# Block transposes on VectorE for the first keys and queries, v in a new token order, and another order of steps

## The chip, the core and the metric

The kernel runs on one core of a Trainium2 chip. The time is the device time of one execution in microseconds; several executions are run and their median is given. A profile is one further execution, recorded instruction by instruction. The core has four compute engines that the text speaks of: TensorE (matmuls, "PE" in the profile, with weight loads as "PEld"), VectorE ("DVE"), ScalarE ("ACT") and GpSimd ("POOL"). SyncE ("SP") issues most DMA transfers, ScalarE and GpSimd issue some.

## The reference

Two layers, one after the other. The first is an attention with polynomial features; the second a feed-forward layer (FFN) whose activation is a ratio of polynomials.

```
batch, n_heads, seq, head_dim = 4, 4, 1088, 32;  r = 8
phi(x):  a = S1 @ x ;  b = S2 @ x ;  outer product of a and b: 64 features
kv  = sum over tokens of phi(k) v^T       (64 x 32 per head)
z   = sum over tokens of phi(k)           (64 per head)
out = (phi(q) kv) / (phi(q) z + 1e-6)     -> x, 4352 tokens x 128

h = x @ w_in                              (128 -> 2048)
P = a0 + a1 h + a2 h^2 + a3 h^3
Q = 1 + |b0| |h| + |b1| h^2
y = (P / (Q + 1e-6)) @ w_out              (2048 -> 128)
```

## The kernel before

**Tiling.** Each of the 4 batches has 1024 main tokens and a remainder of 64. The main tokens of a batch are two chunks of 512 tokens; the remainders of all batches form a last, ninth chunk. A chunk's tokens lie over the 128 partitions with token = 8 p + j, so that a chunk takes four values of j (`JC = 4`).

**Keys, per batch (`add_keys`).** `features` works on one chunk: TensorE transposes four 128x128 f32 tiles of k (one per head, four tokens with their 32 dimensions each; line 420), ScalarE copies the result out of PSUM (line 425), TensorE multiplies with S12, which holds S1 and S2 transposed, in a block-diagonal form (line 430), ScalarE copies a and b out (line 438), VectorE forms the 64 products (line 449). Then TensorE accumulates kv and z over the tokens with v as the other operand (line 466; v has a column of ones for z). After the second chunk and the remainder, VectorE writes kv into block-diagonal form (`kv_bd`, lines 510 and 514) and z into `z_bd` (518); one more matmul with `S2x` (line 523) and two VectorE products (529, 532) turn z into extra columns of the query projection, so that denominators come out of it.

**Queries, per chunk (`add_queries`).** Transposes (555), copy (560), projection (566), copy (577), for all chunks but the first the denominators (588 to 600), the product (605), transposes of the product (613), copy (620) and a matmul with `kv_bd` (626) that gives x transposed. The first chunk is `early`: it doesn't wait for z, but takes numerators and denominators from one set of matmuls (634), divides on VectorE (645 to 655) and transposes x after that (663, 669).

**FFN (`add_group`).** Groups of up to eight blocks of 128 hidden units for one chunk: h in PSUM (line 748), ScalarE copies it to bf16 (`hb`, 754), VectorE and ScalarE form the ratio (the reciprocal of Q as exp(-ln Q), lines 784 and 787), TensorE multiplies with w_out (807). Sixteen groups add some terms by DMAs that accumulate, issued by GpSimd (844). The four groups of kind "s" (4, 7, 11, 15) take |b0| |h| from ScalarE: after each of the four 128x1024 pieces of h is copied, an Abs with scale is run on the same PSUM tile (759).

**Start.** Ten matmuls of zeros keep TensorE busy from the first microsecond (326). SR, S1 and S2 with a copy per head, is loaded to 16 partitions, transposed by TensorE (339), copied by VectorE (347) and masked into S12 (348); `S2x` comes from a matmul with `sel` (343) and a VectorE copy (352). The first batch's k, q and v come in two loads each, 512 bytes in a run; v goes to a spare buffer and GpSimd copies it into `v_aug[0]` (404).

**Order.** Every piece of work is a step of a plan. The list `ORDER` gives the order in which all steps issue their instructions, and so the order on each engine and each DMA queue; waits between engines follow from the data and the buffers. A DMA of SP also waits for the landing of the one issued eight before it (ScalarE's loads at the start count too).

## Time and profile before

| | us |
|---|---|
| median of 3 runs | 268.0 (266.77 to 268.14) |
| the profiled execution's own time | 270.2 |
| its span, first to last instruction | 268.5 |
| TensorE busy | 246.2 (92%) |
| VectorE busy | 244.1 (91%) |
| ScalarE busy | 242.7 (90%) |
| GpSimd busy | 38.2 (14%) |
| first FFN matmul starts | 20.51 |
| last compute instruction ends | 264.5 |

A row of instructions gives start, duration, engine, line, operation, the tiles written and read, shapes and a count, and in brackets the idle time before it with what ended it. A row of the groups by form ends with the group's busy time, the mean of one in ns, and the idle time before. A row of a stage gives its bounds and length, the busy time of TensorE, its weight loads, VectorE, ScalarE and GpSimd, TensorE's granted clock as a share of the full one, the DMA engines' busy share and GB/s.

### The profile page before, as it was taken

The page shows a single profiled execution, that of the slowest core. Times are in us where ns is not written, and L with a number is a line of the kernel's source. Part 1 is how long each engine was busy: PE and PEld are TensorE (multiplying, and loading weights), DVE is VectorE, ACT ScalarE, POOL GpSimd, SP SyncE. Part 2 cuts the span into 40 slices and gives each one's busy share as a digit, 9 for nine tenths or more (in the row PEclk, how much of TensorE's full clock was granted, in tenths as well). Part 3 has the DMA queues.
Part 4 walks back from the last instruction along what each step waited for, and adds up shares of the span by engine and source line. Part 5 has one row for each costly group of instructions (what it writes and reads, how often), then busy time and mean ns, then how long its engine had stood idle before and what let it go on. Part 6 is the DMA issues. An engine that isn't in the chain of part 4 may idle for free.

```text
span 268.5 us, 2984 instructions
## 1 busy us (share of the span) xinstructions
PE 246.2 (92%) x1099; PEld 137.5 (51%) x1113; DVE 244.1 (91%) x234; ACT 242.7 (90%) x218; POOL 38.2 (14%) x58
## 2 busy tenths in 40 slices
PE   8999999999999999999999989999999879778653
PEld 4974567755665645466546434445344334634241
DVE  1643999799999999999999999999999999999992
ACT  2437978899999999999999999999999999999972
POOL 4800001100202101202020302020211202101000
PEclk9997999999999999999999999999999999997995
DMA  6797849980394996296949893959599799897511
GB/s 183 200 294 150 152 100 201 177 172 2 42 114 53 105 171 136 44 121 68 124 76 121 143 172 34 123 88 110 64 123 186 121 138 116 117 99 111 64 39 61
DMA packets 38718, 31.66 MB, mean 118 GB/s; under 512 B 16816, under 2 KB 34992, under 8 KB 38576
## 3 DMA queue, kind: packets, MB, share of 16 engines
q0 software_dynamic: 14144, 20.45, 58.9%
q1 hardware_dynamic: 23792, 10.89, 16.0%
q10 hardware_dynamic: 768, 0.14, 0.3%
q8 instruction: 9, 0.15, 0.2%
q14 instruction: 5, 0.04, 0.0%
HBM read 8.79 MB, written 2.23 MB: 41 GB/s over the span
## 4 chain that ended last, share of the span: by engine, by line
PE 42%; DVE 23%; ACT 23%; issue 6%; DMA 4%; DVEq 0%; ACTq 0%; POOLq 0%
PE h_ps L748 20%; DVE y L780 11%; ACT hb L754 8%; ACT u L787 6%; ACT L L784 5%; PE out_ps L807 5%; PE kv_ps L466 5%; DMA u<-lin 4%; DVE u L780 3%; PE w_ps L430 2%; DVE lin L861 2%; PE out_ps L326 2%; DVE lin L776 2%; DVE y L791 1%; PE w_ps L626 1%
## 5 line engine op out<-in xcount | busy, mean ns | idle before, releaser
L748 PE MATMUL h_ps<-xT,w_in_sb 128*128 128x512 f32 (+1 forms) x288 | 128.3, 581 | 3.8 <-ACT hb L754 3.1
L748 PEld LDWEIGHTS h_ps<-xT,w_in_sb 128*128 128x128 f32 x288 | 52.3, 192 | 54.5 <-issue 40.4
L754 ACT CAST hb<-h_ps 128x1024 bf16<-128x1024 f32 (+1 forms) x70 | 73.6, 1067 | 2.3 <-PE h_ps L748 1.9
L780 DVE TENSOR_TENSOR y<-y,hb 128x4096 bf16<-128x4096 bf16 (+3 forms) x42 | 70.3, 1686 | 0.1
L784 ACT ACTIVATE L<-u,one_ap 128x4096 f32<-128x4096 bf16 (+3 forms) x23 | 66.8, 2906 | 2.4 <-DVE u L780 1.4
L787 ACT ACTIVATE u<-L 128x4096 bf16<-128x4096 f32 (+3 forms) x23 | 64.7, 2812 | 0.1
L780 DVE TENSOR_TENSOR y<-y,u 128x4096 bf16<-128x4096 bf16 (+3 forms) x23 | 40.0, 1739 | 0.2
L807 PEld LDWEIGHTS <-w_out 128*128 128x128 bf16 x224 | 22.1, 100 | 35.0 <-issue 15.0
L844 POOL DMA_DIRECT2D y<-zeros x12 | 19.3, 1612 | 128.1 <-DVE y L780 82.3
L807 PE MATMUL out_ps<-y,w_out 128*128 128x512 bf16 x124 | 30.5, 379 | 0.9 <-DVE y L780 0.5
L780 DVE TENSOR_TENSOR u<-lin,u 128x4096 bf16<-128x4096 bf16 (+3 forms) x19 | 30.8, 1622 | 0.1
L807 PE MATMUL out_ps<-u,w_out 128*128 128x512 bf16 x86 | 23.0, 401 | 4.9 <-ACT o_sb L812 2.7
L791 DVE TENSOR_SCALAR y<-hb,a_sb 128x4096 bf16<-128x4096 bf16 (+3 forms) x19 | 19.3, 1013 | 2.9 <-ACT hb L754 1.9
L776 DVE TENSOR_SCALAR lin<-u,b_abs 128x4096 bf16<-128x4096 bf16 (+3 forms) x19 | 19.2, 1011 | 0.0
L771 DVE TENSOR_SCALAR u<-hb 128x4096 int16<-128x4096 int16 (+3 forms) x19 | 16.9, 890 | 2.2 <-ACT hb L754 2.2
L759 ACT ACTIVATE u<-h_ps,b_abs 128x1024 bf16<-128x1024 f32 x16 | 18.4, 1152 | 0.0
L466 PEld LDWEIGHTS kv_ps<-v_aug,k_p 128*128 128x128 f32 x128 | 15.2, 192 | 1.4 <-DVE y L780 0.8
L466 PE MATMUL kv_ps<-v_aug,k_p 128*128 128x66 f32 x128 | 15.4, 271 | 0.0
L620 ACT COPY q_pT<-w_ps 128x512 f32<-128x512 f32 (+1 forms) x18 | 11.5, 647 | 2.7 <-PE w_ps L613 2.7
L844 POOL DMA_DIRECT2D u<-lin x4 | 5.2, 1311 | 52.7 <-DVE lin L865 26.3
L613 PEld LDWEIGHTS w_ps<-ident,q_p 128*128 128x128 f32 x68 | 8.2, 143 | 8.0 <-ACT q_pT L620 3.6
L449 DVE TENSOR_TENSOR k_p<-ab 128x1024 f32<-128x1024 f32 x8 | 9.6, 1224 | 2.5 <-ACT ab L438 2.5
(100 smaller groups left out, 222.8 us busy)
## 6 DMA issues: line engine op xcount, KB each, us to landing
y<-zeros POOLq DMA_DIRECT2D x11, 1024.0 KB, 11.6
u<-lin POOLq DMA_DIRECT2D x4, 1024.0 KB, 8.3
y<-lin POOLq DMA_DIRECT2D x4, 1024.0 KB, 8.4
out_dram<-oT SPq DMA_DIRECT2D x8, 256.0 KB, 2.4
kq<-in_k_dram SPq DMA_DIRECT2D x3, 512.0 KB, 7.7
v_aug<-in_v_dram SPq DMA_DIRECT2D x12, 128.0 KB, 5.7
kq<-in_q_dram SPq DMA_DIRECT2D x3, 512.0 KB, 4.6
w_in_sb<-in_moe_w_in_dram SPq DMA_DIRECT2D x1, 1024.0 KB, 6.3
```

The costliest lines, as they stand in the source:

```text
L466: nc.tensor.matmul(T["kv", b][:, hp * 66:(hp + 1) * 66], lhsT=lhs(hp), rhs=rhs(hp), start=(first and hp == 0), stop=final, skip_group_chec ...
L748: nc.tensor.matmul(T["h", g, s][:, i * W:(i + 1) * W], lhsT=w_in_sb[:, fi * 128:(fi + 1) * 128], rhs=T["xT", n][:, :W], start=True, stop=True)
L754: nc.scalar.copy(out=T["hb", g][:, s * W:(s + nsub) * W], in_=T["h", g, s][:, :nsub * W])
L759: nc.scalar.activation(out=T["u", g][:, s * W:(s + nsub) * W], in_=T["h", g, s][:, :nsub * W], func=ACT.Abs, scale=b_abs[:, 0:1] if square ...
L771: nc.vector.tensor_scalar(out=u().bitcast(mybir.dt.int16), in0=hb().bitcast(mybir.dt.int16), scalar1=0x7FFF, scalar2=None, op0=AX.bitwise_and)
L776: nc.vector.tensor_scalar(out=lin(), in0=u(), scalar1=b_abs[:, 1:2], scalar2=b_abs[:, 0:1], op0=AX.mult, op1=AX.add)
L780: return lambda: nc.vector.tensor_mul(out=out(), in0=in0(), in1=in1())
L784: nc.scalar.activation(out=T["L", g, l0][:, :lw], in_=T["u", g][:, l0:l0 + lw], func=ACT.Ln, bias=one_ap)
L787: nc.scalar.activation(out=T["u", g][:, l0:l0 + lw], in_=T["L", g, l0][:, :lw], func=ACT.Exp, scale=-1.0)
L791: nc.vector.tensor_scalar(out=y(), in0=hb(), scalar1=a_sb[:, 3:4], scalar2=a_sb[:, 2:3], op0=AX.mult, op1=AX.add)
L807: nc.tensor.matmul(T["o", n][:, :W], lhsT=W_terms[w][:, fis[i], :], rhs=T[src, g][:, i * W:(i + 1) * W], start=(start and i == 0), stop=(s ...
L844: nc.gpsimd.dma_start(out=dst(), in_=src(), accum_op=AX.add, max_dma_last_dim=4096)
```

## The change

- In batches 0 and 1 (`HALVED`) a chunk is 512 consecutive tokens, loaded on its own. Within a key chunk of these, and a query chunk of batch 0 (`Q_BLOCKS`), one VectorE instruction transposes all 32x32 blocks of the loaded tile straight into `kT` or `qT`; TensorE's transposes and ScalarE's copies of those chunks are gone. The projections then give the tokens in another order, partition = token modulo 128.
- v of these batches is loaded in that order, one load per head and chunk: eight loads per batch of 64 KB each, in runs of 128 bytes, straight into `v_aug`; GpSimd's copies are gone. The first two stores of the output write in that order.
- S1 and S2 are loaded to all 128 partitions and transposed by VectorE; `S2x` is a GpSimd copy. `mask4` is made first.
- Nine matmuls of zeros in place of ten at the start, and two and one more behind the two transposes of the first x (`XWARM`).
- In the groups of kind "s", Abs runs once over the whole 128x4096 `hb` in place of four times over PSUM; `hb` is free only after it.
- `ORDER` is a new list. Among other things the first query load is issued ahead of v's, the z projection stands before the first numerators and the second query projection before the first FFN matmul on TensorE; on VectorE the second chunk's denominators and query product come before the first FFN work.

```diff
+    XWARM = (2, 1)
+    ZEROS = 9
+    HALVED = (0, 1)
+    Q_BLOCKS = (0, 1)
...
-    SR = consts.tile([2 * R, H, D], FP, name="SR")
+    SR = consts.tile([128, 2, D], FP, name="SR")
...
+        if b in HALVED:
+            c = part
+            src = src[b, :, c * CW:(c + 1) * CW, :]
+            if name == "v_sb":
+                for h in range(H):
+                    QUEUE[eng].dma_start(out=v_aug[b % 2][:, h, c * JC:(c + 1) * JC, 0:D],
+                                         in_=src[h].rearrange("(a m) d -> m a d", a=JC))
+                return
...
+            QUEUE[eng].dma_start(out=T[name, b][:, :, c * JC:(c + 1) * JC, :],
+                                 in_=src.rearrange("h (p j) d -> p h j d", j=JC))
...
-    ld["v", 0] = load("SP", lambda e: load_main(e, "v_sb", v, 0, 0), 256, rank=-97, take=["q_p"])
-    ld["q", 0] = load("SP", lambda e: load_main(e, "q_sb", q, 0, 0), 256, rank=-96.8, take=["kq"])
-    ld["v", 0, 1] = load("SP", lambda e: load_main(e, "v_sb", v, 0, 1), 256, rank=-96.6)
+    ld["q", 0] = load("SP", lambda e: load_main(e, "q_sb", q, 0, 0), 256, rank=-97, take=["kq"])
+    ld["v", 0] = load("SP", lambda e: load_main(e, "v_sb", v, 0, 0), 512, H, rank=-96.8, take=["v_aug"])
+    ld["v", 0, 1] = load("SP", lambda e: load_main(e, "v_sb", v, 0, 1), 512, H, rank=-96.6)
...
     def s_spread():
-        nc.vector.tensor_copy(out=sT, in_=T["sT"][:, :2 * R])
...
+        nc.vector.transpose(out=sT.rearrange("p s d -> p (s d)"), in_=SR.rearrange("p s d -> p (s d)"))
...
     def s_expanded():
-        nc.vector.tensor_copy(out=S2x, in_=T["s2"][:, :128])
+        nc.gpsimd.tensor_copy(out=S2x, in_=SR[:, 1, None, :].broadcast_to([128, H, D]))
...
+            def block_transposes():
+                T["kT", key] = tile_of(att, "kT", [128, CW], FP)
+                half = T["k_sb", b][:, :, key[1] * JC:(key[1] + 1) * JC, :]
+                nc.vector.transpose(out=T["kT", key].rearrange("p (h m j) -> p h j m", h=H, j=JC), in_=half)
...
+            warm(XWARM[t])
...
+        def s_abs():
+            T["u", g] = tile_of(moe, "u", [128, GW], BF)
+            nc.scalar.activation(out=T["u", g][:, :gw], in_=T["hb", g][:, :gw], func=ACT.Abs, scale=b_abs[:, 0:1])
...
-            p = plan.add("DVE", tt, mul(y, y, hb), after=[p], rank=g - 0.3, give=["hb"], name=f"n2 {g}")
+            p = plan.add("DVE", tt, mul(y, y, hb), after=[p, ha], rank=g - 0.3, give=["hb"], name=f"n2 {g}")
```

## The prediction

> **What bounds the kernel now.** I read the page's engine shares first (TensorE 92%, VectorE 91%, ScalarE 90%: no engine has much room), then the busy time by stage, to see where each engine still has room.

> ```profile
> core 0: us, PE busy (x) PEld busy (x) DVE busy (x) ACT busy (x) POOL busy (x), PEclk, DMA share, GB/s
> 0.00:20.51 20.51, 18.94 (x121) 14.38 (x121) 8.07 (x20) 7.11 (x15) 8.79 (x38) 1.00 0.84 224
> 20.51:27.00 6.49, 6.49 (x16) 3.26 (x17) 2.82 (x8) 4.49 (x6) 0.00 (x0) 0.74 0.70 151
> 27.00:50.00 23.00, 22.89 (x124) 15.44 (x126) 20.99 (x35) 19.95 (x30) 2.53 (x2) 1.00 0.76 149
> 50.00:60.00 10.00, 9.84 (x47) 6.17 (x46) 9.63 (x16) 9.38 (x7) 0.00 (x0) 1.00 0.97 194
> 60.00:150.00 90.00, 89.71 (x395) 50.16 (x400) 89.41 (x69) 89.77 (x80) 11.71 (x8) 1.00 0.70 89
> 150.00:245.00 95.00, 85.15 (x302) 40.18 (x308) 94.88 (x60) 95.00 (x69) 13.86 (x9) 0.99 0.88 119
> 245.00:264.50 19.50, 13.20 (x102) 7.94 (x101) 18.34 (x32) 17.00 (x17) 1.29 (x1) 0.94 0.33 57
> 264.50:268.50 4.00, 0.00 (x0) 0.00 (x0) 0.00 (x0) 0.02 (x1) 0.00 (x0) 0.50 0.21 64
> ```

> The first number of a row is its length, the fourth VectorE's busy time. From 60 to 245 us VectorE idles 0.7 of 185 us. Nearly all its idle time, 24.4 of 268.5 us, lies at the start: 12.4 before the first FFN matmul (20.51), 3.7 up to 27, 2.0 up to 50, then 0.4 + 0.7 + 1.2 and the 4.0 of the last store. So I use a ledger: span = VectorE's work + VectorE's idle time. Work taken from ScalarE or TensorE alone shortens nothing from 60 us on; work given to VectorE lengthens it, unless it fills an early hole.

> The order of time shows what sets the start:

> ```profile
> 0.85 4.43 PE L326 MATMUL out_ps<-const-float32-0.0 128*128 128x512 bf16 x10 [0.85 <-PEq L1019]
> 5.42 1.76 PE L420 MATMUL w_ps<-ident,kq 128*128 128x128 f32 x8
> 6.57 1.24 ACT L425 COPY kT<-w_ps 128x512 f32<-128x512 f32 x2 [4.48 <-PE w_ps L420]
> 7.21 1.10 PE L430 MATMUL w_ps<-S,kT 128*128 128x64 f32 x8
> 8.76 1.23 DVE L449 TENSOR_TENSOR k_p<-ab 128x1024 f32<-128x1024 f32 x1 [2.18 <-ACT ab L438]
> 16.09 0.29 DVE L510 TENSOR_TENSOR kv_bd<-kv_ps,mask 128x128 f32<-128x128 f32 x1 [2.88 <-PE kv_ps L466]
> 17.72 0.17 DVE L645 TENSOR_SCALAR den<-w_ps 128x8 f32<-128x8 f32 x1 [0.77 <-PE w_ps L634]
> ```

> TensorE transposes the keys after its ten warm-up matmuls, ScalarE copies them out, and only at 7.21 does the projection start; the key sums end at 16.06, x is ready and the first FFN matmul starts at 20.51.

> Rows for costs come from the groups by form:

> ```profile
> L333 DVE MEMSET zeros<- 128x512 f32 x1 | 0.5, 485 | 0.1
> L605 DVE TENSOR_TENSOR q_p<-abc 128x512 f32<-128x512 f32 x1 | 0.7, 690 | 0.0
> L449 DVE TENSOR_TENSOR k_p<-ab 128x1024 f32<-128x1024 f32 x8 | 9.6, 1224 | 2.5 <-ACT ab L438 2.5
> L759 ACT ACTIVATE u<-h_ps,b_abs 128x1024 bf16<-128x1024 f32 x16 | 18.4, 1152 | 0.0
> L787 ACT ACTIVATE u<-L 128x4096 bf16<-128x4096 f32 x15 | 56.0, 3737 | 0.0
> ```

> **The change, part by part.**

> *VectorE's work.* Six block transposes of 128x512 f32 are added (four key chunks, two query chunks). The trace has none. Bounds: 0.485 us (the memset of as many elements) and 1.224 us (the product that writes twice as many). I take 0.69, the f32 product of the same 512 elements, since a transpose too reads and writes each element once. Sum 4.1 us. The S2x copy (0.29) leaves VectorE; sT's copy becomes a small transpose (0.17 to about 0.22). Work: 244.1 + 4.1 - 0.29 + 0.05 = 248.0 us.

> *Other engines.* TensorE loses 24 transposes (six groups of four at 0.44 on the chain, 2.6 us) and the two small matmuls from SR, and gains net two warm-up matmuls. ScalarE loses six copies of about 0.6 us and trades 16 x 1.152 = 18.4 us of Abs from PSUM for 4 x 3.74 = 15.0 us from SBUF (priced by the 4096-wide Exp): 7.1 us in all. GpSimd loses the two v copies (0.61 and 1.40). All of it lies beside a full VectorE: worth 0 in the ledger, though it guards VectorE against waits. If VectorE were not full there, ScalarE's 7.1 us would count. The merged Abs is a new wait for the accumulate-DMA behind it on GpSimd's queue and for VectorE's y*hb: for group 4 I put its end near 40 us, and VectorE's own scaled square, which the same DMA needs, near 41, so it hides; if it came late, the DMA (10.5 us on the chain here) would be late by as much, and Ln after it, but VectorE has other groups to work on. The stores of the first two chunks go in 512-byte rows in place of 2 KB, beside work.

> *Start, up to the key sums.* S comes in 256 packets in place of 64; issued by 1.8, with a landing of 2.4 (k's first half took 3.0 with far more bytes) it is there at 4.2, and with transpose and mask product S12 near 4.7 (6.03 before). Then on VectorE: two key transposes (to 5.4 and 6.1) and the query transpose, which waits for a load that takes the place of v's first half in SP's queue; that one let SP go on at 7.18 here, so about 6.8 to 7.5. Were q later, the first key product, queued behind it on VectorE, and with it the key sums would be late by as much. Projections on TensorE 5.6, 6.7, 7.8 to 8.9 (1.10 each); ScalarE's evictions 0.4; VectorE's products 7.5, 8.7, 9.95 to 11.2 (1.23 each). Key sums need v in 128-byte packets: loads one to four are issued by about 5, and land by 8; five to eight queue behind the landing of q (about 6.5) and cost some 0.55 each, so the last is issued near 8.5 and lands near 11. The first half of the sums runs 9 to 11, the second with the remainder's transpose, projection and product and one q_p transpose to about 14.9: 1.1 us earlier than 16.06.

> *Up to the first FFN matmul.* Queued ahead of the first division on VectorE now: the second query transpose (0.69), the two z spreads (0.28 + 0.18), the constants (0.48). It starts near 17.2, against 17.72. On TensorE the z projection (0.30) stands before the numerators and the second query projection (1.03) with a warm-up matmul before the FFN: FFN start at 17.2 + 2.8 (as before) + 0.65 not hidden = 20.65, no earlier. w_in, now behind sixteen loads on SP, not ten, is issued near 11.5 rather than 8.64; with its 6.3 us it lands near 18, a cover of about 2.5 us. If that went, each microsecond counts in full. The w_out casts and the key transposes of batch 1 come 3 to 8 us after w_in's use and have more.

> *What is won.* VectorE resumes at about 21.6 with the second chunk's denominators (0.29, 0.30, 0.25, 0.28) and product (1.22), which now fill the 3.7 us of holes; the first hb is out by 22.5. By 21.6 it has done 8.07 - 0.68 + 4 x 0.69 + 0.46 = 10.6 us, so it idled 11.0 (12.4 before). I follow its new order to 42 us without a hole: 3.7 becomes 0. Of the 2.0 up to 50 I keep 1.5.

> Sum: 248.0 + 11.0 + 0 + 1.5 + 0.4 + 0.7 + 1.2 + 4.0 = 266.8, against 268.5: -1.7 us. The profiled execution took 270.2 us, its span 268.5; the three runs have a median of 268.0, 0.8% below the profiled one, so I subtract the difference from the median: about 266.3 us, -0.6%.

> [...]

> **Rivals.**
> 1. *The transposes are dear (slower).* VectorE is full, so each counts in full. At 1.224, the upper row, the sum grows by 6 x 0.53 = 3.2 to 269.5; it turns slower than before from 0.98 us each (1.7 / 6 above 0.69). [...]
> 2. *v comes late.* The rows by microsecond show what packet size does:

> ```profile
> 3.00:4.00 1.00, 1.00 (x4) 0.39 (x3) 0.00 (x0) 0.00 (x0) 0.47 (x3) 1.00 1.02 295
> 22.00:23.00 1.00, 1.00 (x2) 0.34 (x1) 0.00 (x0) 0.93 (x2) 0.00 (x0) 0.50 0.92 144
> ```

> With DMA full in both, 512-byte packets move 295 GB/s and batch 1's 128-byte v loads 144. v's 512 KB take 3.6 us, not 1.8, and the queue behind them shifts. If the last landing slips from 11 to 13.5, the sums, x and everything after slip 2.5: 268.8; with a slip of 4 it is 270.3, and over 3.0 decides for slower. Against it: most of v is issued 3 us before its use.
> 3. *More is won.* If TensorE's clock (0.50 at 21 to 24 us before) stays up, q lands early and the division starts at 16 with the FFN at 19.4, another 1.5 to 2.5 is won: 264.3. The clock alone gives nothing while VectorE has the denominators to do.
> 4. *It comes to nothing.* The new order opens VectorE holes of 1.5 to 4 us after 27 us, where it had 4.3 us in all: 268 to 270.5. For it: ScalarE and TensorE were as full as VectorE from 60 to 150 us. Against it: ScalarE has 7 us more room.

> **How the numbers follow.** Half a percent, 1.3 us, is about what a measurement of this kernel tells from no change: faster below 266.7, slower above 269.3. The forecast, 0.45: 266.3, by itself 265.0 (transposes at 0.485) to 267.5, of which 0.30 is faster and 0.15 the same. Rival 1, 0.14: 0.04 the same, 0.10 slower. Rival 2, 0.14: 0.06 and 0.08. Rival 3, 0.17: faster. Rival 4, 0.10: 0.04 and 0.06. Faster 0.47, same 0.29, slower 0.24. The range goes from just under rival 3's time (263.6: a bit under 0.1 left out) to 269.8, which holds dear transposes and most of a late v, and leaves out 0.1 above.

> **What would show it.** In the changed profile: the six transposes near 0.69 each; the first key projection near 5.6, the key sums' end near 14.9, the FFN's start near 20.7, denominators straight after; VectorE's busy time near 248 with under 20 us idle; ScalarE's near 235. It is wrong if a transpose is over 1 us, if VectorE waits for q, v or w_in past these times, or if VectorE has holes after 27 us that it did not have.

## The result: 2.9% slower, and the profile after

The changed kernel takes 275.4 us in the median (275.1 to 276.6), the kernel before 267.8 us (266.8 to 268.1). The ratio is 1.029, with a 95% interval from 1.025 to 1.034. The forecast was 266.3 us, in a range from 263.6 to 269.8. The sign is wrong and the time lies outside the range.

The busy time by stage, in the stretches shown for the kernel before (the length, then TensorE, its weight loads, VectorE, ScalarE, GpSimd, the granted clock, the DMA engines' share and GB/s):

```profile
core 0: us, PE busy (x) PEld busy (x) DVE busy (x) ACT busy (x) POOL busy (x), PEclk, DMA share, GB/s
0.00:20.51 20.51, 17.68 (x79) 14.58 (x80) 8.05 (x14) 3.37 (x7) 4.63 (x36) 0.71 0.77 192
20.51:27.00 6.49, 5.87 (x27) 5.14 (x27) 3.25 (x11) 0.96 (x2) 0.00 (x0) 0.50 0.89 147
27.00:50.00 23.00, 22.80 (x111) 14.86 (x110) 20.05 (x37) 18.13 (x24) 0.04 (x1) 0.95 0.49 104
...
60.00:150.00 90.00, 89.58 (x397) 51.22 (x402) 89.44 (x69) 89.90 (x71) 10.86 (x7) 1.00 0.74 100
```

The clock column is the news. In the first stretch it is 0.71 where it was 1.00, and in the second 0.50 where it was 0.74. After 50 us VectorE is full, as it was. So the time was lost before 30 us. The same window in order of time:

```profile
0.85 4.00 PE L343 MATMUL out_ps<-const-float32-0.0 128*128 128x512 bf16 x9 [0.85 <-PEq L1050]
5.19 0.25 DVE L356 STREAM_TRANSPOSE sT<-SR 128x64 f32<-128x64 f32 x1 [5.19 <-DMA SR<-in_S_dram]
5.68 2.01 DVE L421 STREAM_TRANSPOSE kT<-kq 128x512 f32<-128x512 f32 x2
6.83 2.06 PE L436 MATMUL w_ps<-S,kT 128*128 128x64 f32 x16 [1.98 <-DVE kT L421]
10.51 5.33 PE L477 MATMUL kv_ps<-v_aug,k_p 128*128 128x66 f32 x24
20.10 0.29 DVE L521 TENSOR_TENSOR kv_bd<-kv_ps,mask 128x128 f32<-128x128 f32 x1 [2.16 <-PE kv_ps L477]
21.71 3.68 PE L645 MATMUL w_ps<-kv_bd,q_pT 128*128 128x66 f32 x16 [0.40 <-ACT q_pT L631]
28.98 2.52 PE L769 MATMUL h_ps<-xT,w_in_sb 128*128 128x512 f32 x5
29.74 0.29 DVE L599 TENSOR_TENSOR den<-abc 128x128 f32<-128x128 f32 x1 [3.44 <-ACT abc L588]
```

The zeros end at 4.85, the first projection starts at 6.83, and TensorE is idle for 1.98 us between them. In the kernel before, key transposes ran there from 5.42. Twenty-four key sums now take 5.33 us, 0.22 each. kv_bd comes at 20.10 where it was 16.09, the FFN starts at 28.98 where it was 20.51, and VectorE takes up the denominators at 29.74.

The granted clock changes at 5.27 (to full), 8.69 (to half) and 29.17 (to full). From the first of them to the second is once 3.41 us, and to the third seven times, so I cut the start into such windows:

```profile
5.27:8.69 3.42, 1.86 (x16) 1.87 (x16) 3.32 (x6) 0.37 (x1) 2.41 (x13) 1.00 0.82 125
8.69:12.10 3.41, 3.41 (x18) 3.38 (x17) 3.06 (x3) 0.74 (x2) 0.00 (x0) 0.50 0.57 118
12.10:15.51 3.41, 3.41 (x18) 3.41 (x18) 0.77 (x2) 0.00 (x0) 0.00 (x0) 0.50 0.79 188
15.51:29.17 13.66, 13.04 (x58) 11.97 (x59) 4.08 (x14) 2.29 (x6) 0.00 (x0) 0.50 0.95 229
```

In the window with the gap TensorE is busy 1.86 of 3.42 us, and the clock falls at its end. It then stays at half for 20.5 us although TensorE is busy nearly without a break. (Ahead of the first change the column prints 1.00 too, but a zero matmul takes 0.43 us there, and in run 1 the last eight of fourteen, issued about or after the change, take 1.79 us together. So the column is to be read from the first change on.)

VectorE's waits and the costly new forms:

```profile
DVE sT L356 <- DMA SR<-in_S_dram: 5.2, 1, 5.2
DVE k_p_rem L455 <- ACT ab L447: 4.6, 1, 4.6
DVE den L599 <- ACT abc L588: 3.4, 1, 3.4
...
DVE kv_bd L521 <- PE kv_ps L477: 2.2, 1, 2.2
```

```profile
L784 ACT ACTIVATE u<-hb,b_abs 128x4096 bf16<-128x4096 bf16 x4 | 15.2, 3799 | 0.0
...
L421 DVE STREAM_TRANSPOSE kT<-kq 128x512 f32<-128x512 f32 x4 | 4.2, 1090 | 0.0
```

All of VectorE's long waits but the first are for results of TensorE at half clock, two of them by way of a ScalarE copy. A block transpose takes 1.09 us, not 0.69.

### The profile page after: what moved, and what is told of

It reads as the page before. It is cut to its first block, busy times and chain, and to the rows that moved or that the text cites. A ratio compares the mean times of both kernels' runs of the same rounds, so it can differ in the third digit from the quotient of the medians.

```text
span 273.5 us, 2939 instructions
## 1 busy us (share of the span) xinstructions
PE 248.5 (91%) x1075; PEld 142.1 (52%) x1088; DVE 249.5 (91%) x239; ACT 237.1 (87%) x200; POOL 35.7 (13%) x56
## 4 chain that ended last, share of the span: by engine, by line
PE 46%; DVE 44%; issue 5%; ACT 2%; DMA 1%; DVEq 0%; ACTq 0%
DVE y L804 20%; PE h_ps L769 19%; PE kv_ps L477 8%; PE out_ps L831 7%; DVE lin L800 4%; DVE y L815 4%; DVE u L804 3%; DVE u L795 3%; PE w_ps L577 3%; PE w_ps L436 2%; PE w_ps L624 2%; DVE lin L887 2%; PE w_ps L637 2%; DVE q_p L616 1%; PE w_ps L645 1%
## 5 line engine op out<-in xcount | busy, mean ns | idle before, releaser
L769 PE MATMUL h_ps<-xT,w_in_sb 128*128 128x512 f32 (+1 forms) x288 | 126.5, 574 | 2.9 <-ACT hb L775 1.9
L804 DVE TENSOR_TENSOR y<-y,hb 128x4096 bf16<-128x4096 bf16 (+3 forms) x42 | 69.6, 1672 | 0.0
L477 PEld LDWEIGHTS kv_ps<-v_aug,k_p 128*128 128x128 f32 x128 | 18.2, 227 | 1.6 <-DVE k_p L455 0.8
L477 PE MATMUL kv_ps<-v_aug,k_p 128*128 128x66 f32 x128 | 18.8, 310 | 0.0
L870 POOL DMA_DIRECT2D u<-lin x4 | 6.3, 1564 | 74.8 <-PE kv_ps L477 41.7
L784 ACT ACTIVATE u<-hb,b_abs 128x4096 bf16<-128x4096 bf16 x4 | 15.2, 3799 | 0.0
L624 PEld LDWEIGHTS w_ps<-ident,q_p 128*128 128x128 f32 x68 | 8.9, 151 | 7.9 <-issue 4.6
L624 PE MATMUL w_ps<-ident,q_p 128*128 128x128 f32 x68 | 11.2, 292 | 1.6 <-ACT q_pT L631 1.6
## 6 DMA issues: line engine op xcount, KB each, us to landing
y<-zeros POOLq DMA_DIRECT2D x11, 1024.0 KB, 11.5
```

What stands on the lines that cost most here:

```text
L477: nc.tensor.matmul(T["kv", b][:, hp * 66:(hp + 1) * 66], lhsT=lhs(hp), rhs=rhs(hp), start=(first and hp == 0), stop=final, skip_group_chec ...
L624: nc.tensor.transpose(T["qpTp", n, hp][:, i * 128:(i + 1) * 128], in_=qp[:, i, hp * 128:(hp + 1) * 128], identity=ident)
L769: nc.tensor.matmul(T["h", g, s][:, i * W:(i + 1) * W], lhsT=w_in_sb[:, fi * 128:(fi + 1) * 128], rhs=T["xT", n][:, :W], start=True, stop=True)
L804: return lambda: nc.vector.tensor_mul(out=out(), in0=in0(), in1=in1())
L870: nc.gpsimd.dma_start(out=dst(), in_=src(), accum_op=AX.add, max_dma_last_dim=4096)
```

## The experiments

The theory after the result, drawn from changes that lie 3.41 us, or seven times that, apart: TensorE's clock is decided at such intervals by what TensorE did in the interval before. The block transposes moved work off TensorE at the one place where that work kept the clock up. What ran on TensorE at half clock in the start then took nearly twice as long (the 24 key sums 5.33 us for 2.95 in the kernel before, the 16 matmuls with kv_bd 3.68 for 1.97). The rivals: the block transposes cost VectorE too much; v's eight loads, the moved loads or the new order cost the time; the merged magnitudes block ScalarE. All kernels below compute the whole reference.

**1. More zeros, nothing else.**

```diff
-    ZEROS = 9
+    ZEROS = 14
```

> The changed kernel with 14 zero matmuls at the start in place of 9, so that TensorE is not idle between 4.85 and the first key projection near 6.8 us. Theory A (the idle gap lets TensorE's clock fall to 0.50 from 8.7 to 29.2 us, and that doubles the matmuls of the attention): the clock is up from about 7 us, the key sums end near 15 us instead of 20, the first FFN matmul starts near 21 instead of 29, the time is 267 to 270 us. Theory B (the six block transposes at 1.09 us each and the new order are the loss, the clock only goes along): 274 to 276 us.

Measured: 267.75 us (267.0 to 274.3, ten executions), ratio 0.9999 (0.9975 to 1.0024). The profile's span is 266.1 us against 273.5. Rows of its start, in order of time:

```profile
6.74 2.03 PE L436 MATMUL w_ps<-S,kT 128*128 128x64 f32 x16 [1.34 <-DVE kT L421]
9.69 2.86 PE L477 MATMUL kv_ps<-v_aug,k_p 128*128 128x66 f32 x24
15.05 0.29 DVE L521 TENSOR_TENSOR kv_bd<-kv_ps,mask 128x128 f32<-128x128 f32 x1 [0.89 <-PE kv_ps L477]
21.65 3.71 PE L769 MATMUL h_ps<-xT,w_in_sb 128*128 128x512 f32 x8
22.36 0.29 DVE L599 TENSOR_TENSOR den<-abc 128x128 f32<-128x128 f32 x1 [2.51 <-ACT abc L588]
```

The same 24 key sums take 2.86 us and kv_bd comes at 15.05, with the same block transposes, loads and order as the changed kernel. The clock is full from 3.61 on, but for one window:

```profile
17.27:20.68 3.41, 3.19 (x15) 2.63 (x16) 1.61 (x6) 0.37 (x1) 0.00 (x0) 0.50 1.08 290
```

Five zero matmuls give back 7.6 us, so the loss hangs on the clock. One of the ten executions took 274.3 us. It has no profile; its mean clock of 0.964, where the other nine have 0.975 to 0.993, suggests that fourteen zeros don't hold the clock every time.

**2. The old kernel without its zeros.**

```diff
-        warm(10)
+        warm(1)
```

> The kernel before with one zero matmul in place of ten, nothing else changed. Theory A: without the warm-up its clock stays at 0.50 through the first attention work too; the first FFN matmul starts at 26 to 29 us rather than 20.5 and the time is 272 to 276 us. Theory B: the zero matmuls only delay the first transposes, so the time is 266 to 268.5 us.

Measured: 278.8 us (277.8 and 279.8), ratio 1.040 (1.033 to 1.047). That is slower than the 276 us at most that were expected. The first grant of the full clock comes at 32.21, the FFN starts at 29.24, and the wait for the key sums grows, in VectorE's waits:

```profile
DVE kv_bd L510 <- PE kv_ps L466: 7.7, 2, 7.0
```

It was 2.88 at its longest. The old kernel depends on the clock in the same way, so the effect does not come with the new layout.

**3. The merged magnitudes in the old kernel, in the place of the last of the four.**

```diff
-            nc.scalar.activation(out=T["u", g][:, s * W:(s + nsub) * W], in_=T["h", g, s][:, :nsub * W], func=ACT.Abs,
-                                 scale=b_abs[:, 0:1] if square else 1.0)
+            if square:
+                if (s, nsub) == subs[-1]:
+                    nc.scalar.activation(out=T["u", g][:, :gw], in_=T["hb", g][:, :gw], func=ACT.Abs, scale=b_abs[:, 0:1])
+                return
```

> The kernel before with the one Abs over 128x4096 from SBUF in place of four over PSUM in the four groups of that kind, at the place of the last of the four; nothing else changed. If VectorE alone bounds the time from 60 us on: 0 to 1 us from before (ScalarE 3 us less busy, no gain). If ScalarE is a bound beside it: 2 to 4 us faster. If the later end of the merged Abs delays its group: 1 to 3 us slower.

Measured: 279.2 us (277.5 to 280.0, four executions), ratio 1.040 (1.034 to 1.047). The rows of the first merged magnitude on ScalarE and of the stages behind it:

```profile
35.55 3.72 ACT L761 ACTIVATE u<-hb,b_abs 128x4096 bf16<-128x4096 bf16 x1
```

```profile
27.00:50.00 23.00, 20.60 (x101) 13.11 (x101) 19.74 (x31) 16.26 (x22) 1.33 (x1) 0.93 0.72 139
50.00:60.00 10.00, 9.95 (x63) 7.81 (x64) 7.29 (x12) 9.70 (x12) 1.20 (x1) 1.00 0.86 148
60.00:150.00 90.00, 87.95 (x383) 49.62 (x388) 87.49 (x68) 84.86 (x69) 10.35 (x7) 1.00 0.68 91
```

```profile
37.70:41.11 3.41, 1.31 (x12) 1.32 (x12) 3.38 (x4) 2.79 (x4) 1.33 (x1) 1.00 0.29 103
```

One Abs of 3.72 us holds ScalarE's queue at a stroke where four of 1.15 us let copies through between them. Behind it the copies of kT, the second batch's projections and the FFN's copies are late, and VectorE idles 3.3 us from 27 to 50 us (2.0 in the profile before), 2.7 up to 60 (0.4), 2.5 up to 150 (0.6) and 3.7 up to 245 (0.1). The clock has a part in it: TensorE waits 2.35 us for a late copy of kT, up to 39.80, the window from 37.70 to 41.11 (the last row) holds 1.31 us of its work, and the next one runs at half clock. The expected 1 to 3 us were too little. The changed kernel, with the same four instructions of 3.80 us each, shows no such holes (0 idle from 50 to 60 us, 0.56 up to 150). So the merged form needs an order that fits it. What it is worth under that order was not measured by itself.

**4. Fourteen zeros, and the second batch's keys back on TensorE.**

```diff
-    ZEROS = 9
+    ZEROS = 14
+    K_BLOCKS = (0,)
...
-                s = plan.add("DVE", 600, block_transposes, after=after + [before], rank=rank, take=["kT"], give=give,
+                s = plan.add("DVE", 600, block_transposes if key[0] in K_BLOCKS else tensor_transposes, after=after + [before], rank=rank, take=["kT"], give=give,
```

`tensor_transposes` stands for the four transposes and ScalarE's copy of before, in the same step; v of that batch comes in the old token order.

> As the run with 14 zero matmuls, and the two key chunks of batch 1 are transposed by TensorE and copied by ScalarE again (v of that batch then in the old order within a chunk, still in eight loads). If VectorE is the bound, its two transposes of 1.09 us cost in full: 2 to 2.5 us faster than the run with 14 zero matmuls alone. If they lie beside other work: 0 to 0.5 us from it, or slower by the 1.2 us that ScalarE and TensorE get.

Measured: 268.3 us (268.05 to 271.1, ten executions), ratio 1.0031 (1.0003 to 1.0059), beside 267.75 for the run with fourteen zeros alone. VectorE's busy time falls from 249.4 to 247.9 us, but new waits appear among its waits:

```profile
DVE y L810 <- ACT u L817: 1.9, 1, 1.9
```

Taking two transposes (2.2 us) off VectorE gains nothing, since VectorE then waits for ScalarE. The forecast's "each counts in full" does not hold in that direction under this order.

This profile also shows the start without the half-clock window of run 1. The work up to the FFN is the same, and the granted clock stays full from 4.36 on:

```profile
20.68 3.71 PE L775 MATMUL h_ps<-xT,w_in_sb 128*128 128x512 f32 x8
21.39 0.29 DVE L605 TENSOR_TENSOR den<-abc 128x128 f32<-128x128 f32 x1 [2.19 <-ACT abc L594]
```

The FFN and the denominators start 1.0 us earlier than in run 1.

**5. All six block transposes back on TensorE, nine zeros.** The edit is that of run 4 for the keys of both batches and the two query chunks of the first; the first two stores go back to the old token order, and step 64, the first key half, stands one place later in the list.

```diff
-            s = plan.add("DVE", 600, block_transposes, after=load_steps + [T.get(("q tr", n - 1)) if give else None], rank=rank, take=["qT"], give=give,
+            s = plan.add("DVE", 600, tensor_transposes, after=load_steps + [T.get(("q tr", n - 1)) if give else None], rank=rank, take=["qT"], give=give,
```

> The changed kernel with its nine zero matmuls, its order, its loads and its merged magnitudes, but with the six 32x32-block transposes (keys of the first two batches, queries of the first) put back on TensorE with a ScalarE copy in the same places of the order; v and the two first stores go back to the (partition, slot) order of tokens. The clock theory: the gap of 1.98 us on TensorE between the zeros' end (4.85) and the first key projection (6.83) is filled by eight transposes and shortened, so the granted clock stays full past 8.7, the key sums end at 15 to 16 and not at 20.05, and the time is 265 to 269 us. The rival, that something else of the change costs the 7 us (the eight v loads, the moved loads, the order): still 273 to 276 us although no block transpose is left in the start.

Measured: 281.6 us (281.5 to 282.1), ratio 1.050 (1.046 to 1.054), a miss. The windows of the clock show why:

```profile
3.84:7.26 3.42, 3.04 (x23) 2.31 (x21) 0.47 (x2) 1.17 (x2) 1.47 (x9) 1.00 1.06 190
7.26:10.67 3.41, 0.13 (x2) 0.00 (x0) 0.00 (x0) 0.27 (x1) 0.94 (x6) 1.00 0.53 82
10.67:34.56 23.89, 23.53 (x102) 21.52 (x103) 7.62 (x18) 4.70 (x12) 0.00 (x0) 0.50 0.78 187
```

The first window, with the transposes in the gap, keeps the clock. The second has TensorE idle but for 0.13 us, and the clock falls at its end and stays down for 23.9 us. I had made that gap myself. The load of the remaining keys, which ScalarE issues, now stood behind its copies, went out only at 9.04, after SP's eight v loads and two more, and ScalarE's next eviction came only at 10.40. Run 10 mends it.

**6. The first key half ahead of S on VectorE, nine zeros.**

```diff
-    ..., 52, 4, 53, 3, 6, 8, 10, 13, 64, 51, ...
+    ..., 52, 4, 64, 53, 3, 6, 8, 10, 13, 51, ...
```

> The changed kernel with nine zeros; the one edit is that VectorE transposes the first half of the keys before S and not behind it. The key half lands near 3.7 and S at 5.19, so the first projection can start near 6.0 instead of 6.83 and the gap on TensorE is some 1.2 us instead of 1.98. The clock theory: if 1.2 us is short enough for the clock, about 267 us, the clock full past 8.7; if it is not, 274 to 276 with the half clock until about 29 as before. Should the clock have nothing to do with the gap, the earlier projection is worth its own 0.8 us and no more: 274.5.

Measured: 274.3 us (274.0 to 276.0), ratio 1.024 (1.019 to 1.028). The first projection starts at 5.71, and the windows are:

```profile
3.78:7.19 3.41, 2.09 (x15) 1.53 (x14) 3.08 (x5) 0.34 (x1) 1.47 (x9) 1.00 1.01 196
7.19:27.67 20.48, 20.08 (x92) 18.80 (x91) 8.56 (x19) 3.07 (x9) 2.93 (x6) 0.50 0.88 210
```

A projection 1.1 us earlier does not save the clock. The forecast had it at 5.6: about at its own start time, then, the clock falls. The zeros ended at 4.39 here, since the last ones ran at full clock, so the gap was 1.32 us.

**7. Eleven zeros.**

```diff
-    ZEROS = 9
+    ZEROS = 11
```

> The changed kernel with eleven zero matmuls instead of nine: the zeros end near 5.7 and the gap up to the first key projection at 6.8 is 1.1 us instead of 1.98. Together with the run that moves the keys ahead of S this tells what length of gap the clock bears: about 267.8 us (as with fourteen zeros) if 1.1 us is borne, 274 to 276 if not. A mixture of both over the runs would say that it depends on where the gap falls against the times at which the clock is granted.

Measured: 275.5 us (274.1 to 276.5), ratio 1.027 (1.022 to 1.031). The zeros end at 5.48, the projection starts at 6.96 after 1.48 us of idling (the 1.1 us that the run was meant for did not come about), and the clock falls at 8.54. With fourteen zeros the idle time was 1.34 us, hardly shorter, and the clock held. So the length of the gap alone does not decide. Compare the window of run 1 that holds its gap with that of run 6 above:

```profile
3.61:7.03 3.42, 2.08 (x11) 0.88 (x9) 1.81 (x4) 0.00 (x0) 1.28 (x7) 1.00 1.10 215
```

TensorE is busy 2.08 us in the one and 2.09 in the other. In run 1 these are nearly all zeros of 512 columns (1.8 us), and the clock stays; in run 6 they are 0.6 us of zeros and 1.5 us of projections 64 columns wide, and it falls.

**8. An attempt at a better version:** fourteen zeros, the first key half ahead of S, no zeros among the transposes of x, the second query projection ahead of the second of them.

```diff
-    XWARM = (2, 1)
-    ZEROS = 9
+    XWARM = (0, 0)
+    ZEROS = 14
...
-            T["abcp", n] = tile_of(aps, "w_ps", [128, CW], FP)
+            T["abcp", n] = warm_ps[0] if n == 1 else tile_of(aps, "w_ps", [128, CW], FP)
```

> A version that might beat both kernels: the changed kernel with fourteen zeros, the first key half transposed ahead of S, no zero matmuls among the transposes of x, and the projection of the second query half (which the denominators wait for) ahead of the second transposes of x instead of behind them, in the accumulator of the zeros. With fourteen zeros VectorE waited 2.51 us for that projection's eviction, until 22.36. If the wait is worth its length, denominators start at 20.7 to 21.2 and the time is 265.5 to 266.8 us (1.2 us less from the projection, up to 0.8 from the keys). If the start of the feed-forward part (21.65) sets the pace instead, it is 267.5 to 268.5.

Measured: nine executions, four from 265.8 to 268.2 us and five from 269.9 to 270.5; the ratio of 0.993 (0.988 to 0.998) is that of the first four alone. The profile is of one of the five:

```profile
13.03:16.44 3.41, 3.11 (x24) 2.66 (x24) 2.18 (x8) 1.29 (x3) 0.00 (x0) 1.00 0.83 224
16.44:26.68 10.24, 9.78 (x31) 6.75 (x31) 6.12 (x17) 2.60 (x6) 0.00 (x0) 0.50 0.96 227
```

Here 3.11 us of narrow work in 3.41 did not keep the clock, and it stays down for three windows. (In run 4 a window with 3.12 us of the same kind of work, from 14.60 to 18.02, did keep it.) In run 1 a window like it (3.12 us busy) dropped the clock as well, but the zeros among x's transposes stood in the next one, and it came back after 3.41 us. So the zeros that I took out seem to have been doing work; run 11 puts some back.

**9. Twelve zeros in the middle of the low stretch.**

```diff
+            warm(12 if n == 0 else 0)
```

(behind the matmuls of the first query projection, in the changed kernel)

> The changed kernel with its nine zero matmuls at the start and twelve more behind the first query projection, near 10.5 us, in the middle of the 20 us of half clock. In the changed kernel TensorE was 3.41 of 3.41 us busy with small f32 matmuls in the stretches 8.7 to 12.1 and 12.1 to 15.5 and the granted clock stayed at 0.50. Theory: the low clock holds itself, because small f32 matmuls don't raise it however busy they keep TensorE, and zero matmuls do (0.85 to 4.85 raised it in every run). Then the clock comes back to full at 15.5 or 18.9 instead of 29.2, the zeros cost about 5 us of TensorE's time and the rest of the start runs at twice the rate: feed-forward start at 26 to 28 instead of 28.98 and 272 to 274.5 us. Rival: any busy stretch raises it and something else (a fixed time after the fall, or the wide f32 matmuls of the feed-forward alone) decides: clock still at half until about 29 to 34, and 278 to 281 us.

Measured: 273.9 us (272.9 to 275.5), ratio 1.026 (1.023 to 1.029). The windows:

```profile
8.26:11.67 3.41, 3.41 (x17) 3.29 (x17) 2.96 (x3) 0.77 (x3) 0.30 (x2) 0.50 0.52 87
11.67:15.08 3.41, 3.41 (x9) 1.21 (x8) 1.71 (x2) 0.35 (x1) 0.00 (x0) 0.50 0.71 147
15.08:18.50 3.42, 3.42 (x29) 3.06 (x28) 0.00 (x0) 0.00 (x0) 0.00 (x0) 1.00 0.99 364
```

Both half-clock windows are busy throughout. The first holds seventeen matmuls, nearly all narrow, and changes nothing; the second holds zeros, and full clock follows at 15.08, as expected and not at 29 or later. The FFN starts at 26.64. The low clock held itself here: 3.41 us of nearly all narrow f32 matmuls didn't end it, 3.41 us of zeros of 512 columns did. In run 2 no zeros were needed for that: the clock came at 32.21, after the first window in which most of the time went to the FFN's 512-column f32 matmuls (from 29.24).

**10. Run 5 with the load of the remaining keys ahead of ScalarE's copies.**

```diff
-    ..., 10, 13, 51, 64, 55, 70, 11, 12, ...
+    ..., 10, 13, 51, 11, 64, 55, 70, 12, ...
```

> The run with all six block transposes back on TensorE again, with one move: ScalarE issues the load of the remaining keys ahead of its copies of the transposed keys. In the first version that issue stood behind the copies, was made only at 9.04, behind SP's eight v loads and two more, held ScalarE 4.29 us (first projection's eviction at 10.40) and left TensorE idle from 7.4 to 10.8, so a second gap took the clock, which the first window had kept (full from 3.84 to 10.67). With the gap gone the clock theory says: full until 17 or later, the feed-forward start near 21, and 266 to 270 us. If the clock still falls before 12, the block transposes are not what opens the gap, and the time is 274 us or more.

Measured: 268.6 us (268.3 to 269.1, ten executions), ratio 1.0035 (1.0017 to 1.0052). The first windows of the clock, and the engine shares:

```profile
3.73:7.14 3.41, 3.02 (x23) 2.33 (x21) 0.47 (x2) 1.35 (x3) 1.38 (x8) 1.00 0.96 198
7.14:10.56 3.42, 3.40 (x31) 3.18 (x29) 2.99 (x3) 1.52 (x4) 3.11 (x6) 1.00 0.58 91
```

```profile
PE 243.0 (91%) x1099; PEld 136.5 (51%) x1112; DVE 244.7 (92%) x233; ACT 240.5 (90%) x206; POOL 37.7 (14%) x56
```

With nine zeros and the transposes on TensorE the clock stays full from 3.73 to 246 us in the profile, and none of the ten executions is slower than 269.1. In run 5, without the moved load, the first window kept the clock too. So it was the block transposes that opened the gap. VectorE does 4.7 us less here than in run 1 (244.7 against 249.4) and the time is no better (268.6 against 267.75).

**11. Run 8 with zeros put back.**

```diff
-    XWARM = (0, 0)
+    XWARM = (1, 0)
...
+            warm(2 if b == 0 else 0)
```

(two behind the z projection; the early projection's eviction also moves ahead of the second copy of x)

> The version with fourteen zeros, keys ahead of S and the second query projection early, mended in two places: two zero matmuls behind the small projection of the denominators' weights (where TensorE waits) and one behind the first transposes of x, and the early projection's eviction ahead of the copy of x. Without them the stretch 13.0 to 16.4 let the clock fall and, with no zero matmuls among the transposes, it stayed at half until 26.7 (269.9 us, where executions that kept it gave 265.8). Expected: the clock full through the start in most executions and 265 to 266.5 us; 269 to 270 if the clock falls again.

Measured: 266.7 us (265.5 to 268.7, twelve executions), ratio 0.9954 (0.9925 to 0.9984). That is just above the 265 to 266.5 expected. None of the twelve went to 270.

**12. Fourteen zeros, the first key half ahead of S, two zeros behind the z projection; the second query projection where the change has it.**

```diff
-    ZEROS = 9
+    ZEROS = 14
...
+            warm(2 if b == 0 else 0)
```

(and the move of step 64 as in run 6)

> The changed kernel with fourteen zeros, the first key half transposed ahead of S, two zeros behind the small projection of the denominators' weights, and the second query projection where the change has it. Beside the run with the projection early this tells what that move is worth: 266.8 to 267.8 us (267.75 with fourteen zeros alone, less up to 0.8 for the keys).

Measured: 266.35 us (265.9 to 267.6, nine executions), ratio 0.9955 (0.9934 to 0.9977), a little faster than expected. Three rows of its start:

```profile
5.73 2.13 PE L403 MATMUL w_ps<-S,kT 128*128 128x64 f32 x16 [0.27 <-DVE S L324]
14.16 0.29 DVE L488 TENSOR_TENSOR kv_bd<-kv_ps,mask 128x128 f32<-128x128 f32 x1 [0.88 <-PE kv_ps L444]
20.42 0.29 DVE L567 TENSOR_TENSOR den<-abc 128x128 f32<-128x128 f32 x1 [2.19 <-ACT abc L556]
```

This version and run 11 beat the kernel before by just under half a percent, and the changed kernel with it. The gain over run 1 (1.4 us) comes with a start 0.9 us (kv_bd) to 1.9 us (denominators) earlier. About 1.0 of the 1.9 us goes with run 1's half-clock window, which this profile does not have (run 4 starts its denominators at 21.39 without it). What the keys and what the two zeros gave was not measured apart. The early query projection of run 11 adds nothing to it that the intervals can tell.

## Why the prediction was wrong

**The step that failed** is "All of it lies beside a full VectorE: worth 0 in the ledger", said of the 24 transposes that TensorE loses. Eight of them stood in the one stretch where VectorE was not full and where nothing else kept TensorE at work. Without them the window from 5.27 to 8.69 held 1.86 us of work, the clock went to half, and it stayed there to 29.17. The forecast knew the clock as something that might stay up (rival 3) and held that "the clock alone gives nothing while VectorE has the denominators to do". None of its rivals was a clock that falls. Runs 1, 9 and 10 show the cause from three sides: more zeros before the gap, zeros after it, no gap.

**Start times.** The forecast took the rates of full clock throughout: 1.10 us for a projection, key sums ended at 14.9, division from 17.2, FFN at 20.65, VectorE back at 21.6. Measured were 20.0, 23.7, 28.98 and 29.74 for the last four. In run 1 they are 14.9, 17.35, 21.65 and 22.36, with half clock from 17.27 to 20.68. In run 4, with the clock full throughout the start, they are 15.0, 17.44, 20.68 and 21.39, each within 0.25 us of the forecast. So the path was read rightly for a full clock. Some of that is luck: the first projection started at 6.74 in run 1, not at 5.6, and the key sums still ended on time, so the forecast's steps between were 1.1 us too slow.

**The ledger.** Forecast were 248.0 us of work and 18.8 of idling, a span of 266.8. The changed kernel has 249.5 and 24.0, a span of 273.5. In run 1 it is 249.4 and 16.7, a span of 266.1. The sum came out to 0.7 us once the clock was nearly as it assumed, but by errors that cancel: 1.4 us too little work against 2.1 us too much idling.

**From the span to the time.** A second step failed on size. Run 1 takes 267.75 us and not 266.3. I had taken off the 2.2 us by which the profiled execution of the kernel before lay over its median. Run 1's profiled execution lies at its own median (267.84), so there was nothing to take off. Beside the experiments the kernel before ran 59 times, with spans from 265.0 to 268.5 us and 266.2 in the middle; the profiled span of 268.5 stands at the upper end. The gain of 1.7 us was a gain over an execution at that end. With the clock held in the first windows the change comes to no difference, which the forecast gave 0.29.

**The transposes' price (rival 1).** 1.09 us each, over the 1 us that the forecast named as a sign of being wrong, within the bounds of 0.485 and 1.224 but near the upper one: 6 x 0.40 = 2.4 us more than the term of the sum (VectorE's work as a whole came out 1.5 us above the forecast). But run 10, with no block transpose, is no faster than run 1, so rival 1's "VectorE is full, so each counts in full" did not bear out: with less work VectorE waited more (run 4).

**S.** It reached VectorE's transpose at 5.19, not 4.2, which lengthened the gap. Run 6, where the first projection started at 5.71 in place of 6.83, shows that this did not decide.

**Rivals 2 and 4.** No wait of the changed kernel's profile is for v or w_in; v was issued up to 8.3 us and w_in at 11.44, as forecast. No holes opened after 30 us (0.2 us of idling up to 50). The merged magnitudes under the new order hid, as forecast; under the old order they cost 11.5 us (run 3), so "worth 0" for ScalarE's relief was right only together with the list.

**What was right:** VectorE's work to 1.5 us (the transposes 2.4 us over, the rest 0.9 us under), ScalarE's at 237.1 (forecast near 235), the 3.7 us of holes behind the FFN's start, which are nearly gone once the clock holds, and VectorE's being full from 50 to 245 us.

## What to carry to other kernels

Work that looks free on an engine "with room" may be what keeps TensorE's clock up, as the eight key transposes did here (run 10). Before taking matmuls or transposes off TensorE in a latency-bound start, cut its timeline into the windows at which the granted clock changes and see what remains in each. Narrow f32 matmuls kept a full clock in every profile here only where they filled a window (3.40 of 3.42 us in run 10), and did not raise a low one at 3.41 of 3.41 us, so a gap of 1.3 to 2 us with few wide matmuls around it cost twenty microseconds at half clock (20.5 in run 6 and in the changed kernel); a few wide zero matmuls ahead of the gap (267.75 us), or the old transposes in it (268.6), cost nothing by comparison with its 275.4. And take a difference between a profiled execution and the median for noise unless the trace shows where it comes from.

## What the runs showed of the hardware that was not expected

```profile
6.98:10.39 3.41, 2.48 (x24) 2.47 (x23) 1.75 (x2) 1.33 (x3) 1.98 (x6) 1.00 0.71 138
```

- At half clock 3.41 of 3.41 us of f32 matmuls with 64 to 66 columns didn't raise it in any run, nor did 3.42 us with 66 to 128 columns in run 8. The windows after which it rose held 512-column matmuls (bf16 zeros, f32 of the FFN). How many it takes isn't shown: 0.86 us of zeros stood in the window before the rise in run 1, and 0.89 us in one of run 5 (27.74 to 31.15) brought none. Which property counts (columns, weight loads between them) stays open.
- Where the windows fall differs from execution to execution (first change at 3.61, 5.27, 5.13, 6.21 us in the profiles of run 1, the changed kernel, runs 7 and 8). That may be why a kernel with one weak stretch has two times: 265.8 and 270 us in run 8, 267.7 and 274.3 in run 1. Only one execution of each was profiled, so it is not shown.
- A 32x32-block transpose of 128x512 f32 took 1.08 us (queries) to 1.09 us (keys) in the mean on VectorE in the changed kernel's profile; one of 128x64 took 0.25.
- A load issued by ScalarE went out only after ten loads that SP had been issuing (9.04 in run 5, where ScalarE was free from 6.1), and ScalarE was idle for 4.3 us up to its next copy. By the trace that idle time ended with the landing of a v load. So it may be the kernel's own rule that a load waits for the landing of the one issued eight before it; this trace does not settle it.
